# An attention and gated-convolution kernel on one core: loads as pieces of the written order, more buffers for them, and a new order for opening, period and end

## The chip, the cores and the metric

The kernel runs on one core of one Trainium2 chip. The metric is the device time of one execution in microseconds (us), lower is better.

## What is computed

```python
scores = q @ k^T / sqrt(64) + bias[head, distance]      # 8 sequences, 8 heads, 576 tokens, head size 64
scores = where(0 <= i - j < 128, scores, -1e9)          # window of 128 tokens back
attn   = exp(scores - max); attn /= sum(attn) + 1e-9
x      = (attn @ v), heads side by side                 # (8, 576, 512)
h      = relu(x @ w_in)                                 # w_in: 512 x 1024
c      = conv over tokens of h, 3 taps per column, zero at the ends of a sequence
out    = (h * sigmoid(c)) @ w_out                       # w_out: 1024 x 512
```

All inputs are float32. The 4608 tokens of the eight sequences are taken as one long row.

## The kernel before

**Units of work.** Tokens are cut into 36 tiles of 128 (index t). A tile's attention looks at the keys of the tile itself and of the one before it. Two tiles make a chunk of 256 tokens, of which there are 18; for each chunk the 1024 hidden columns are done in four steps of 256, so that there are 72 steps (index s). Both big products are made from three matmuls each, with every operand split in a high and a low part. The weights reach the kernel as words that must first be taken apart; there are 17 blocks of them (index b): 0 to 3 and 5 to 8 are the halves of `w_in`, 4 is the small convolution table, 9 to 16 are `w_out`.

**Pieces.** Nothing is left to a scheduler: the order of the instructions is written out as a string of pieces, and each engine runs its instructions in the order in which the pieces name them. A piece has a name, an index, and for some a half. The names, with the engine and the line of the work:

- weights, block b: F (load into a buffer `wst`, the sync engine SP, L152), CL (GpSimd, POOL, L159), RS (ScalarE, ACT, L164), V (VectorE, DVE, three instructions, L170 to L174), H (ACT, L182), P (TensorE, PE, L191 and L192), W (ACT, L196).
- attention, tile t: LD (loads of queries and keys into `rqk`, SP, L228), LV (load of values), Q (PE, transposes, L236), QO (ACT, copy, L240), S0 and S1 (PE, scores of four heads each, L262), MA (DVE, mask and bias, L278 and L291), RM (DVE, row extreme, L295), X (ACT, exponentials, L300), N (DVE, three instructions, L311 to L313), T (PE, transposes of the weights, L320), RL (ACT, L325), SEL (POOL, L331 and L334), AV (PE, L351), XH (ACT, L362), XL (DVE, L366), XF (DVE, the edge columns between chunks, L380 or L382).
- step s, with two halves of 128 columns: UH (PE, first product, 12 matmuls a half, L395), HH (ACT, relu, L403), Z (ACT, middle tap, L409), CV (DVE, the outer taps, L422), TH (ACT, tanh, L429), GT (DVE, gate, L433), GH (ACT, L440), GL (POOL, low part, L445), D (PE, second product, 12 matmuls, L459), OB (ACT copy, L469, and the store on SP, L471; only after the last step of a chunk).

A half is written after a point: N0.1 in the period below is the second half (heads 4 to 7) of the tile of that period. CV takes two instructions for a half, and four in the six chunks in which a sequence begins inside. The tiles in which a sequence begins or ends have one more mask instruction in each MA.

**Buffers.** `wst` has 3 buffers, `rqk` 2, the values 4. In PSUM five buffers (`pst`) are shared by Q, S, T, AV, P and UH; Z, CV and TH work on one buffer (`zp`), so that a step's Z waits for GT of the step before; D sums into two (`o`), which the next chunk can take only when OB has copied them. Z of a step's second half also waits for CV of its first, as both stand in the one buffer.

**Order.** `OPENING` carries tiles 0 to 5, all weights and steps 0 to 5. Then `PERIOD` is emitted once per tile for t = 6 to 39, with two steps each, and pieces whose tile or step does not exist are left out; so the last four rounds (t = 36 to 39) have only what is left: AV of tile 35 and the steps 66 to 71. Loads are not pieces. Eight are issued ahead of `OPENING`, and the others as part of a piece: V of block b issues F of block b + 3 (L177), Q of tile t issues LD of tile t + 2 (L479), AV of tile t issues LV of tile t + 3 (L488). They go into SP's one queue in that order, each waiting there until its buffer is free.

Of the kernel before, what the change touches and what calls it, by code (L numbers as in the profile page):

```python
# [21 lines left out]
def tile_alibi_window_attention_conv_glu(  # L22
# [144 lines left out]
    def w_bits(b):  # L167
        st, g = wst.pop(b), wgs[b]
        lo, hi = st[..., 0], st[..., 1]
        nc.vector.tensor_scalar(out=lo, in0=lo, scalar1=29, scalar2=None, op0=ALU.logical_shift_right)  # L170
        nc.vector.scalar_tensor_tensor(
            out=g, in0=g, scalar=3, in1=lo, op0=ALU.logical_shift_left, op1=ALU.bitwise_or
        )
# [346 lines left out]
    RM0.1 X0.0.0 RS2 H1 CL3 W0 P1 RS3 V2 X0.1.1 V3 S1.0 X0.0.1 X0.1.0 N0.0 MA1.0.0 H3 N0.1 MA1.0.1 T0.0  # L522
    CL4 S1.1 T0.1 RL0.0 RS4 P3 RM1.0 H2 P2 SEL0.0 MA1.1.0 RL0.1 CL6 SEL0.1 MA1.1.1 X1.0.0 X1.0.1 N1.0
    RM1.1 CL5 AV0 W2 T1.0 S2.0 V4 XH0 XL0 X1.1.0 X1.1.1 RL1.0 MA2.0.0 N1.1 RS5 H4 V5 SEL1.0 S2.1 P4 T1.1
    MA2.0.1 MA2.1.0 RM2.0 W3 MA2.1.1 H5 W1 RL1.1 CL7 XF0 SEL1.1 RS6 RS7 AV1 X2.0.0 V6 X2.0.1 W4 RM2.1 P5
    XH1 CL8 X2.1.1 V7 N2.0 Q4 RS8 X2.1.0 Q3 N2.1 V8 CL9 XL1 W5 QO4 XF1 H6 QO3 T2.1 H7 T2.0 P6 RL2.1
    RL2.0 RS9 CL10 S3.0 SEL2.0 SEL2.1 MA3.0.0 P7 S3.1 MA3.0.1 H8 AV2 MA3.1.0 P8 XH2 MA3.1.1 V9 W7 RM3.1
    CL11 XL2 RS10 RM3.0 XF2 UH0.0 RS11 V11 H9 UH1.0 X3.1.1 X3.0.0 V10 X3.1.0 H11 HH0.0 X3.0.1 HH1.0 N3.1
    UH0.1 S4.0 N3.0 MA4.0.0 CL12 Z0.0 T3.0 MA4.0.1 T3.1 HH0.1 CL14 Z0.1 RL3.0 P9 RL3.1 CV0.1 H10 RS12
    SEL3.0 W6 P10 RM4.0 SEL3.1 X4.0.1 AV3 W9 UH1.1 X4.0.0 CV0.0 CL13 P11 V12 N4.0 TH0 RS13 XH3 GT0 H12  # L530
    S4.1 XL3 W8 HH1.1 P12 Z1.0 MA4.1.0 XF3 GH0 Q5 Z1.1 MA4.1.1 UH2.0 CL15 GL0 CV1.1 W12 RM4.1 W10 QO5
    CV1.0 X4.1.0 X4.1.1 TH1 T4.0 V13 UH2.1 RS14 N4.1 HH2.0 H13 D0 GT1 V14 RL4.0 Z2.0 HH2.1 UH3.0 HH3.0
    CV2.0 T4.1 W11 Z2.1 CL16 GH1 CV2.1 RL4.1 P13 S5.0 MA5.0.0 UH3.1 GL1 TH2 GT2 S5.1 RS16 HH3.1 SEL4.1
    SEL4.0 GH2 MA5.1.0 RS15 Z3.0 D1 MA5.0.1 W13 V15 AV4 H14 XH4 Q6 RM5.0 H15 MA5.1.1 QO6 X5.0.0 Z3.1 XL4
    XF4 P15 P14 RM5.1 GL2 W14 X5.0.1 CV3.0 CV3.1 TH3 W15 V16 UH4.0 N5.0 D2 X5.1.1 H16 UH4.1 HH4.0 X5.1.0
# [53 lines left out]
```

## Time and profile before

| what | value |
|---|---|
| median of 3 runs | 698.07 us (697.06 to 699.02) |
| the profiled execution's own time | 697.87 us |
| its span in the trace | 696.1 us |
| TensorE (PE) busy | 654.1 us, 94% of the span |
| VectorE (DVE) busy | 521.1 us, 75% |
| ScalarE (ACT) busy | 444.1 us, 64% |
| GpSimd (POOL) busy | 191.5 us, 28% |
| TensorE clock, mean granted | 0.99 |

The profile is of one execution. A row of its timeline gives the start and the duration in us, the engine, the line, the operation and, in brackets, how long the engine stood idle before it and what ended that. Rows for the same line that follow one another are merged, with their count behind an x. A row of the chain of waits gives start, duration, engine and line of the work that ended last, followed back from the end. A row of the table by stretches gives for each engine the busy time and the instructions, then the granted TensorE clock as a share of full speed, and the DMA share. The profiled execution takes 1.8 us more than its span.

### The profile page before, as it was taken

To read this page: it belongs to the slowest core of one execution; us is meant where nothing else is said; L and a number is where in the kernel's file an instruction comes from. 1 tells how busy PE (TensorE), PEld (TensorE's weight loads), DVE (VectorE), ACT (ScalarE), POOL (GpSimd) and SP (SyncE) were. 2 spreads that over 40 slices of the span, in tenths; PEclk is the share of its full clock that TensorE was granted. 3 is DMA by queue.
4 is the path that set the end of the run, shared out by engine and by line. 5 is a ranking of instruction groups with operands and counts; after the bars stand their busy time and mean duration, and the time that the engine had idled before them with its cause. 6 is when DMAs were issued, how large, how long until landed. Compare 5 with 4: busy or idle time off the path is not lost.

```text
span 696.1 us, 13391 instructions
## 1 busy us (share of the span) xinstructions
PE 654.1 (94%) x4881; PEld 555.6 (80%) x4881; DVE 521.1 (75%) x1207; ACT 444.1 (64%) x1275; POOL 191.5 (28%) x234
## 2 busy tenths in 40 slices
...
GB/s 220 174 79 223 82 59 45 77 47 77 46 76 47 76 46 77 47 76 46 93 36 73 62 61 47 77 46 77 49 74 50 75 46 76 16 32 1 31 30 32
DMA packets 120101, 47.02 MB, mean 68 GB/s; under 512 B 113356, under 2 KB 113380, under 8 KB 120036
## 3 DMA queue, kind: packets, MB, share of 16 engines
...
## 4 chain that ended last, share of the span: by engine, by line
PE 52%; DVE 34%; ACT 8%; issue 3%; DMA 2%; SPq 1%; POOL 1%; ACTq 0%; DVEq 0%; POOLq 0%
PE o L459 18%; PE p L395 13%; DVE zp L422 10%; PE sc L262 7%; PE av L351 7%; DVE sc L278 5%; DVE st L295 4%; DVE e L313 4%; DVE e L291 4%; PE pa L320 3%; ACT zp L409 3%; PE pt L236 2%; DVE x L366 2%; DMA rqk<-in_k_dram 2%; PE pw L191 1%
## 5 line engine op out<-in xcount | busy, mean ns | idle before, releaser
L422 DVE SCALAR_TENSOR_TENSOR zp<-hh,cw,zp 128x256 f32<-128x256 f32 (+7 forms) x384 | 162.0, 422 | 89.8 <-ACT zp L409 81.3
L395 PE MATMUL p<-x,wi 128*128 128x258 f32 x1728 | 224.0, 286 | 2.8 <-DVE x L380 2.8
L395 PEld LDWEIGHTS p<-x,wi 128*128 128x128 f32 x1728 | 215.6, 191 | 8.8 <-issue 5.3
L459 PE MATMUL o<-wo,gh 128*128 128x512 f32 x576 | 188.2, 408 | 3.6 <-ACT ob L469 2.3
L300 ACT ACTIVATE e<-e,st 128x128 f32<-128x128 f32 x288 | 112.0, 391 | 33.7 <-DVE st L295 33.6
L459 PEld LDWEIGHTS o<-wo,gh 128*128 128x128 f32 x576 | 103.4, 189 | 30.5 <-issue 5.6
L445 POOL TENSOR_TENSOR gl<-z,gh 128x512 fp32r<-128x512 f32 x72 | 92.5, 1285 | 114.4 <-ACT gh L440 100.7
L331 POOL TENSOR_SCALAR_AFFINE_SELECT rl<-rl 128x512 f32<-128x512 f32 x64 | 40.6, 635 | 289.2 <-ACT rl L325 289.2
L459 PE MATMUL o<-wo,gl 128*128 128x512 f32 x288 | 114.8, 399 | 1.2 <-POOL gl L445 1.2
L409 ACT ACTIVATE zp<-hh,cw 128x256 f32<-128x256 f32 x144 | 69.1, 480 | 70.6 <-DVE zp L422 67.5
L403 ACT ACTIVATE hh<-p 128x258 f32<-128x258 f32 x144 | 54.7, 382 | 37.9 <-PE p L395 37.8
L433 DVE SCALAR_TENSOR_TENSOR z<-zp,hh 128x512 f32<-128x512 f32 x72 | 49.7, 690 | 34.1 <-ACT zp L429 34.1
L351 PEld LDWEIGHTS av<-rl,rv 128*64 128x64 f32 x1088 | 60.0, 139 | 12.9 <-POOL rl L334 9.2
L351 PE MATMUL av<-rl,rv 128*64 128x128 f32 x1088 | 69.3, 280 | 0.4 <-POOL rl L334 0.4
L262 PE MATMUL sc<-qkT_all 64*128 64x256 f32 x512 | 68.3, 395 | 0.5 <-DVE x L366 0.4
L459 PEld LDWEIGHTS o<-wo,gl 128*128 128x128 f32 x288 | 54.5, 189 | 15.3 <-POOL gl L445 2.1
L291 DVE SCALAR_TENSOR_TENSOR e<-sc,bias 128x256 f32<-128x256 f32 x144 | 61.2, 425 | 4.9
L262 PEld LDWEIGHTS sc<-qkT_all 64*128 64x128 f32 x512 | 48.3, 188 | 19.6 <-ACT zp L409 9.5
L320 PE MATMUL pa<-ident_r,e 128*128 128x128 f32 x288 | 42.5, 277 | 16.4 <-DVE e L313 12.1
L278 DVE COPY_PREDICATED sc<-m_prev,sc 128x256 f32<-128x256 uint8 x128 | 53.7, 420 | 5.2 <-PE sc L262 4.3
L362 ACT CAST x<-av 128x512 fp32r<-128x512 f32 x36 | 21.3, 591 | 56.5 <-PE av L351 56.5
L334 POOL TENSOR_SCALAR_AFFINE_SELECT rl<-rl 128x512 f32<-128x512 f32 x72 | 45.9, 638 | 39.7 <-ACT rl L325 28.8
...
## 6 DMA issues: line engine op xcount, KB each, us to landing
...
```

What stands on the lines that cost most here:

```text
L262: nc.tensor.matmul(pss[a][:, g], qt, qkT_all[rows, win, u, 1, g, :], start=True, stop=True)
L278: nc.vector.copy_predicated(out=s_cur, mask=mask.unsqueeze(1).to_broadcast(shp), data=data)
L291: nc.vector.scalar_tensor_tensor(out=heads, in0=s_cur, scalar=-0.125, in1=b, op0=ALU.mult, op1=ALU.add)
L300: nc.scalar.activation(out=e[:, j, :], in_=e[:, j, :], func=AF.Exp, bias=st[:, 0, j : j + 1], scale=-1.0, accum_out=st[:, 1, j : j + 1],)
L320: nc.tensor.transpose(ps[:, j, :], e[:, j, :], ident)
L351: nc.tensor.matmul(ps[a * D : (a + 1) * D, u * NG + g], vraw[tt][:, u * HU + j], rl[:, side, j], start=n == 0, stop=n == len(sides) - 1,)
L395: nc.tensor.matmul(ps[:, :XW], a[:, cc, f * P : (f + 1) * P], x[:, cc, :], start=n == 0, stop=n == last)
L403: nc.scalar.activation(out=hhs[s][:, ff, :], in_=pts.pop((s, ff, "up"))[:, :XW], func=AF.Relu, scale=0.5)
L409: nc.scalar.activation(out=zps[s][:, ff, :], in_=hhs[s][:, ff, 1 : 1 + CW], func=AF.Copy, scale=cw[:, 1, f : f + 1])
L422: nc.vector.scalar_tensor_tensor(out=z[:, ff, a:cut], in0=hh[:, ff, a + kk : cut + kk], scalar=cw[:, kk, f : f + 1], in1=z[:, ff, a:cut], ...
L445: nc.gpsimd.tensor_tensor(out=gl, in0=zgs.pop(s), in1=as32(gh), op=ALU.subtract)
L459: nc.tensor.matmul(oos[c][m], g[:, ff, ms], w[:, f, :], start=f == 0 and n == 0, stop=f == NFC - 1 and n == 2)
```

## The change

- `wst` gets 6 buffers instead of 3, `rqk` 3 instead of 2.
- F, LD and LV become pieces (`TILE` and `WEIGHT` name them), and V, Q and AV no longer issue any load.
- `OPENING` is another order of the same pieces, with the loads among them. `PERIOD` is another order, too.
- A third string, `TAIL`, is emitted once after the last period and takes the place of the four rounds with missing pieces.

```diff
     wpool = ctx.enter_context(tc.tile_pool(name="wpool", bufs=3))
+    NST = 6
...
-        st = wpool.tile([P, WB, 2], U32, name=f"wst{b}", tag="wst")
+        st = wpool.tile([P, WB, 2], U32, name=f"wst{b}", tag="wst", bufs=NST)
...
-        fetch_weight(b + 3)
...
-        rqk = apool.tile([P, 2, H, D], F32, name=f"rqk{t}", tag="rqk", bufs=2)
+        rqk = apool.tile([P, 2, H, D], F32, name=f"rqk{t}", tag="rqk", bufs=3)
...
-        if t + 2 < NT:
-            load(t + 2)
...
-    def attn_v(t):
-        av(t)
-        if t + 3 < NT:
-            loadv(t + 3)
...
+        "LD": load, "LV": loadv, "Q": qk, "QO": qk_out, "S": scores, "MA": merge, "RM": rowmax,
...
-    Q0 QO0 CL0 S0.0 Q1 MA0.0.0 RS0 MA0.0.1 V0 S0.1 MA0.1.0 RM0.0 MA0.1.1 QO1 CL1 Q2 H0 P0 CL2 QO2 RS1 V1
+    LD0 F0 LD1 LV0 F1 F2 F3 F4 LD2 LV1 F5 Q0 CL0 QO0 S0.0 S0.1 Q1 RS0 MA0.0.0 QO1 MA0.1.0 MA0.0.1
+    MA0.1.1 RM0.0 RM0.1 V0 F6 S1.0 X0.0.1 S1.1 X0.1.0 MA1.0.0 CL2 X0.1.1 N0.1 X0.0.0 T0.1 N0.0 MA1.0.1
...
     PERIOD = """
-    S0.0 S0.1 MA0.0.0 AV-1 MA0.0.1 D-2 OB-2 XH-1 XL-1 GH-1 RM0.0 X0.0.1 XF-1 MA0.1.0 UH0.0 MA0.1.1
-    X0.0.0 RM0.1 N0.0 UH0.1 GL-1 Q1 HH0.0 Z0.0 CV0.0 UH1.0 X0.1.0 HH0.1 Z0.1 X0.1.1 CV0.1 QO1 UH1.1 N0.1
-    T0.0 TH0 HH1.0 GT0 RL0.0 T0.1 HH1.1 SEL0.0 Z1.0 CV1.0 Z1.1 CV1.1 RL0.1 GH0 TH1 SEL0.1 D-1 OB-1 GT1
-    GL0
+    S0.0 S0.1 AV-1 LV2 MA0.0.0 XH-1 D-2 OB-2 MA0.0.1 XL-1 RM0.0 GH-1 X0.0.0 XF-1 UH0.0 X0.0.1 UH0.1
+    MA0.1.0 HH0.0 MA0.1.1 Z0.0 RM0.1 GL-1 UH1.0 CV0.0 HH0.1 X0.1.0 Z0.1 X0.1.1 N0.0 CV0.1 Q1 LD3 T0.0
+    UH1.1 N0.1 HH1.0 TH0 RL0.0 HH1.1 SEL0.0 GT0 Z1.0 T0.1 QO1 CV1.0 Z1.1 RL0.1 CV1.1 SEL0.1 GH0 TH1 GT1
+    GL0 D-1 OB-1
...
+    TAIL = """
+    AV-1 GH-1 XH-1 GL-1 XL-1 XF-1 D-2 OB-2 UH0.0 HH0.0 Z0.0 UH0.1 CV0.0 HH0.1 Z0.1 CV0.1 TH0 GT0 GH0 GL0
+    UH1.0 HH1.0 Z1.0 UH1.1 CV1.0 D-1 OB-1 HH1.1 Z1.1 CV1.1 TH1 GT1 GH1 GL1 UH2.0 HH2.0 Z2.0 UH2.1 CV2.0
...
+    CV5.0 D3 OB3 HH5.1 Z5.1 CV5.1 TH5 GT5 GH5 GL5 D4 OB4 D5 OB5
...
         emit(OPENING)
-        for t in range(FIRST, NT + 4):
+        for t in range(FIRST, NT):
             emit(PERIOD, t, 2 * (t - FIRST) + 6)
+        emit(TAIL, NT, 2 * (NT - FIRST) + 6)
```

Three places show what moves. Rows are instructions in the order of one engine: line, operation, what it writes and what it reads; the line numbers after the change are one or two lower.

The first is the order of VectorE early in the opening, from the second row extreme of tile 0 (`st_1`) on. Before:

```order
L295 TENSOR_REDUCE st_1_200<-e_1_199 128x4
L170 TENSOR_SCALAR wst_139<-wst_139 128x512
L171 SCALAR_TENSOR_TENSOR wg_241<-wg_241,wst_139 128x512
L174 SCALAR_TENSOR_TENSOR wg_241<-wst_139,wg_241 128x512
L170 TENSOR_SCALAR wst_191<-wst_191 128x512
L171 SCALAR_TENSOR_TENSOR wg_249<-wg_249,wst_191 128x512
L174 SCALAR_TENSOR_TENSOR wg_249<-wst_191,wg_249 128x512
L311 TENSOR_SCALAR st_0_181<-st_0_181 128x4
L312 RECIPROCAL st_0_181<-st_0_181 128x4
L313 TENSOR_TENSOR e_0_180<-e_0_180,st_0_181 128x512
L278 COPY_PREDICATED sc_0_0_263<-m_prev,sc_0_0_263 128x2x128
```

After:

```order
L293 TENSOR_REDUCE st_1_196<-e_1_195 128x4
L169 TENSOR_SCALAR wst_130<-wst_130 128x512
L170 SCALAR_TENSOR_TENSOR wg_187<-wg_187,wst_130 128x512
L173 SCALAR_TENSOR_TENSOR wg_187<-wst_130,wg_187 128x512
L276 COPY_PREDICATED sc_0_0_210<-m_prev,sc_0_0_210 128x2x128
L289 SCALAR_TENSOR_TENSOR e_0_226<-sc_0_0_210,bias 128x2x128
L309 TENSOR_SCALAR st_1_196<-st_1_196 128x4
L310 RECIPROCAL st_1_196<-st_1_196 128x4
L311 TENSOR_TENSOR e_1_195<-e_1_195,st_1_196 128x512
L309 TENSOR_SCALAR st_0_190<-st_0_190 128x4
L310 RECIPROCAL st_0_190<-st_0_190 128x4
L311 TENSOR_TENSOR e_0_189<-e_0_189,st_0_190 128x512
```

Before, four weight blocks (V0 to V3, the last two shown) stood ahead of N of tile 0 and MA of tile 1; now one does (V0, block `wst_130`), and MA and N of the two tiles come before V1.

The second is VectorE in one period, from the second row extreme on; `zp` is written by CV, `e` by N. Before:

```order
L295 TENSOR_REDUCE st_1_3646<-e_1_3645 128x4
L311 TENSOR_SCALAR st_0_3600<-st_0_3600 128x4
L312 RECIPROCAL st_0_3600<-st_0_3600 128x4
L313 TENSOR_TENSOR e_0_3599<-e_0_3599,st_0_3600 128x512
L422 SCALAR_TENSOR_TENSOR zp_3699<-hh_3697,cw,zp_3699 128x256 x4
L311 TENSOR_SCALAR st_1_3646<-st_1_3646 128x4
L312 RECIPROCAL st_1_3646<-st_1_3646 128x4
L313 TENSOR_TENSOR e_1_3645<-e_1_3645,st_1_3646 128x512
```

After:

```order
L293 TENSOR_REDUCE st_1_3674<-e_1_3673 128x4
L420 SCALAR_TENSOR_TENSOR zp_3681<-hh_3677,cw,zp_3681 128x256 x2
L309 TENSOR_SCALAR st_0_3619<-st_0_3619 128x4
L310 RECIPROCAL st_0_3619<-st_0_3619 128x4
L311 TENSOR_TENSOR e_0_3618<-e_0_3618,st_0_3619 128x512
L420 SCALAR_TENSOR_TENSOR zp_3681<-hh_3677,cw,zp_3681 128x256 x2
L309 TENSOR_SCALAR st_1_3674<-st_1_3674 128x4
L310 RECIPROCAL st_1_3674<-st_1_3674 128x4
```

N0.0 stood ahead of both halves of CV0; now it stands between them. On PE the period went UH0.0 UH0.1 Q1 UH1.0 UH1.1 T0.0 T0.1 and now goes UH0.0 UH0.1 UH1.0 Q1 T0.0 UH1.1 T0.1.

The third is the end of ScalarE's order, the last two steps (70 and 71). Before:

```order
L403 ACTIVATE hh_7923<-p_0_7892 128x258
L403 ACTIVATE hh_7923<-p_1_7909 128x258
L409 ACTIVATE zp_7928<-hh_7923,cw 128x256 x2
L440 CAST gh_7935<-z_7925 128x512
L429 ACTIVATE zp_7928<-zp_7928 128x512
L440 CAST gh_7966<-z_7951 128x512
L469 COPY ob_0_7982<-o_0_7842 128x512
L469 COPY ob_1_7985<-o_1_7843 128x512
```

After:

```order
L438 CAST gh_7899<-z_7897 128x512
L401 ACTIVATE hh_7916<-p_0_7903 128x258
L407 ACTIVATE zp_7918<-hh_7916,cw 128x256
L401 ACTIVATE hh_7916<-p_1_7920 128x258
L407 ACTIVATE zp_7918<-hh_7916,cw 128x256
L427 ACTIVATE zp_7918<-zp_7918 128x512
L438 CAST gh_7954<-z_7952 128x512
L467 COPY ob_0_7982<-o_0_7878 128x512
```

GH of step 70 (the first `gh` in each) stood behind the middle taps of step 71; now it stands ahead of all of step 71. On PE the end went UH68 UH69 D67 D68 UH70 UH71 D69 D70 D71, and now goes D66 UH69 D67 UH70 D68 UH71 D69 D70 D71.

More of the change, by code (lines that the diff above doesn't have):

```diff
@@ L483, in qk_out @@
             qkT_out(t, u)
-    def attn_v(t):
-        av(t)
-        if t + 3 < NT:
-            loadv(t + 3)
     TILE = {
-        "Q": qk, "QO": qk_out, "S": scores, "MA": merge, "RM": rowmax,
+        "LD": load, "LV": loadv, "Q": qk, "QO": qk_out, "S": scores, "MA": merge, "RM": rowmax,
         "X": lambda t, u, h: exps(t, u, range(2 * h, 2 * h + 2)),
-        "N": normal, "T": attnT, "RL": attn_out, "SEL": select, "AV": attn_v, "XH": x_hi, "XL": x_lo, "XF": xfin,
+        "N": normal, "T": attnT, "RL": attn_out, "SEL": select, "AV": av, "XH": x_hi, "XL": x_lo, "XF": xfin,
     }
@@ L502, in tile_alibi_window_attention_conv_glu @@
     }
-    WEIGHT = {"CL": w_clamp, "RS": w_rebias, "V": w_bits, "H": w_hi, "P": w_rest, "W": w_lo}
+    WEIGHT = {"F": fetch_weight, "CL": w_clamp, "RS": w_rebias, "V": w_bits, "H": w_hi, "P": w_rest, "W": w_lo}
     def emit(pieces, t=0, s=0):
@@ L520, in tile_alibi_window_attention_conv_glu @@
     OPENING = """
-    Q0 QO0 CL0 S0.0 Q1 MA0.0.0 RS0 MA0.0.1 V0 S0.1 MA0.1.0 RM0.0 MA0.1.1 QO1 CL1 Q2 H0 P0 CL2 QO2 RS1 V1
[L522 to L535, printed above, removed]
```

32 lines of the change are left out of this document (20 added, 12 removed).

## The prediction

> **What bounds the kernel now.** First the page, for the engine that is busy most; then the table by stretches, cut where the opening, the steady part and the end meet; then the waits of PE in each stretch.
>
> ```profile
> span 696.1 us, 13391 instructions
> PE 654.1 (94%) x4881; PEld 555.6 (80%) x4881; DVE 521.1 (75%) x1207; ACT 444.1 (64%) x1275; POOL 191.5 (28%) x234
> ```
>
> PE (TensorE) is busy for 94% of the span. The change takes no matmul away, so all that it can win lies in PE's other 42 us and in stretches at a lower clock. In the table the columns behind the stretch are its length and the busy time of PE, of its weight loads, DVE, ACT and POOL, then the granted clock, the DMA share and GB/s.
>
> ```profile
> 0.00:7.90 7.90, 3.36 (x16) 2.37 (x16) 3.17 (x20) 2.46 (x3) 1.60 (x10) 1.00 0.83 194
> 7.90:22.00 14.10, 6.99 (x27) 4.67 (x27) 6.30 (x14) 4.41 (x9) 1.92 (x3) 1.00 1.02 242
> 22.00:65.10 43.10, 32.66 (x192) 19.85 (x191) 37.85 (x82) 29.83 (x91) 12.75 (x19) 0.92 0.56 148
> 65.10:110.50 45.40, 44.32 (x294) 34.94 (x295) 39.56 (x85) 33.55 (x94) 12.69 (x16) 0.96 0.31 88
> 110.50:119.70 9.20, 9.20 (x62) 7.80 (x60) 6.05 (x13) 7.08 (x18) 2.92 (x4) 1.00 0.01 2
> 119.70:642.40 522.70, 512.60 (x4026) 448.22 (x4025) 410.54 (x964) 344.96 (x1019) 148.26 (x175) 1.00 0.24 58
> 642.40:696.10 53.70, 44.97 (x273) 37.72 (x272) 17.61 (x33) 21.79 (x46) 11.33 (x10) 0.97 0.08 30
> ```
>
> PE's idle time: 23.2 us in the opening (the first five rows: 119.7 less 96.5), 10.1 us in the 523 us of the steady part, 8.7 us in the end. DVE is the second engine in the opening: 37.85 of 43.1 us before the first step begins at 65.1. The waits of PE, in the steady part and from 630 us on (total, times, longest):
>
> ```profile
> PE pa L320 <- DVE e L313: 10.1, 19, 0.6
> ...
> PE o L459 <- ACT ob L469: 2.3, 1, 2.3
> PE o L459 <- ACT gh L440: 1.3, 2, 0.7
> PE o L459 <- POOL gl L445: 1.2, 2, 0.6
> ```
>
> The steady part has one kind of wait, T for N, in 19 tiles. So there are three separate sums.
>
> **The end (the tail order).** Here is what one wait costs, and how long a step takes from HH to the low part that D needs:
>
> ```profile
> 671.79 0.73 PE L459 MATMUL o<-wo,gh 128*128 128x512 f32 x2 [2.30 <-ACT ob L469]
> 673.66 1.06 PE L459 MATMUL o<-wo,gh 128*128 128x512 f32 x2
> 677.88 0.39 ACT L403 ACTIVATE hh<-p 128x258 f32<-128x258 f32 x1 [5.14 <-PE p L395]
> 679.93 0.48 ACT L409 ACTIVATE zp<-hh,cw 128x256 f32<-128x256 f32 x1 [0.22 <-DVE zp L422]
> 684.59 0.48 ACT L409 ACTIVATE zp<-hh,cw 128x256 f32<-128x256 f32 x1 [1.14 <-DVE zp L422]
> 687.56 0.62 ACT L440 CAST gh<-z 128x512 fp32r<-128x512 f32 x1 [0.83 <-DVE z L433]
> 688.26 1.30 POOL L445 TENSOR_TENSOR gl<-z,gh 128x512 fp32r<-128x512 f32 x1 [1.30 <-ACT gh L440]
> ```
>
> D68 starts a new chunk right behind D67 and waits 2.30 us for OB; then its pairs of matmuls take 1.06 us where they take 0.63 elsewhere, for nine more matmuls, some 1.8 us. Together with the other waits (1.3 + 1.2) and 0.15 us of refilling behind each of five, the end loses 2.3 + 1.8 + 2.5 + 0.7 = 7.3 us. In the new order a pair of UH stands between each two D up to D69, so OB of D67 is done under UH70, and the waits at D66, D68 and D70 go. What is late next: ACT, DVE and the one `zp` buffer. A step now runs alone, HH to GH. From HH of the first half to Z of the second is 679.93 − 677.88 = 2.05 us, from there to GH 687.56 − 684.59 = 2.97, GH itself 0.62: a step every 5.65 us. PE needs a UH pair and a D for each, 2.88 + 2.81 = 5.7 us (the chain's rows, below), so the two keep pace, but GH of a step stands ahead of HH of the next on ACT, and the chain begins late: UH67 follows UH66 at once. Counted on from there (end of UH66 = 0): GH66 ends at 4.3, HH67 starts then, HH71 at 4.3 + 4 × 5.65 = 26.9, its GH at 31.9, its low part is ready at 26.9 + 2.05 + 2.97 + 0.70 + 1.30 = 33.9. PE is through D70 at 31.3 (five more UH pairs, six D). So D71 waits 0.7 us for GH and about 1.4 more for GL: 2.1 us. The end gains 7.3 − 2.1 = **5.2 us** (7.3 if the chain is not late, 3.5 if it slips by half a microsecond more in each of the last steps).
>
> **The period.** One of the tiles whose CV takes four instructions, and, below the dots, one with the additional mask (its second RM, CV and T):
>
> ```profile
> 283.78 3.04 PE L395 MATMUL p<-x,wi 128*128 128x258 f32 x24
> 285.72 0.16 DVE L311 TENSOR_SCALAR st<-st 128x4 f32<-128x4 f32 x1
> 285.84 0.48 ACT L409 ACTIVATE zp<-hh,cw 128x256 f32<-128x256 f32 x1
> 286.13 0.69 DVE L313 TENSOR_TENSOR e<-e,st 128x512 f32<-128x512 f32 x1
> 286.66 1.03 PE L236 MATMUL pt<-ident_r,rqk 128*128 128x128 f32 x8
> 286.74 1.52 DVE L422 SCALAR_TENSOR_TENSOR zp<-hh,cw,zp 128x192 f32<-128x192 f32 x4
> 287.45 3.13 PE L395 MATMUL p<-x,wi 128*128 128x258 f32 x24
> 288.35 0.48 ACT L409 ACTIVATE zp<-hh,cw 128x256 f32<-128x256 f32 x1 [0.96 <-DVE zp L422]
> 288.86 1.53 DVE L422 SCALAR_TENSOR_TENSOR zp<-hh,cw,zp 128x192 f32<-128x192 f32 x4 [0.60 <-ACT zp L409]
> 291.55 0.63 PE L320 MATMUL pa<-ident_r,e 128*128 128x128 f32 x4 [0.53 <-DVE e L313]
> ...
> 250.38 0.69 DVE L295 TENSOR_REDUCE st<-e 128x4 f32<-128x512 f32 x1
> 253.61 1.01 DVE L422 SCALAR_TENSOR_TENSOR zp<-hh,cw,zp 128x256 f32<-128x256 f32 x2 [0.60 <-ACT zp L409]
> 255.78 0.63 PE L320 MATMUL pa<-ident_r,e 128*128 128x128 f32 x4 [0.56 <-DVE e L313]
> ```
>
> T0.1 waits for N0.1, and N0.1 comes behind CV0.0, Z0.1 and CV0.1. In the new order CV0.0 no longer waits for N0.0: it can start when Z0.0 is done (286.32 + 0.04) and ends at 287.9; N0.0 follows (from 285.72 to 286.82 before, some 1.05 us in a row) to 288.9, under which Z0.1 runs; CV0.1 starts at 288.9. Before, it started at 288.86. In these 12 tiles nothing changes: the 0.6 us in which DVE waited for Z are filled by N0.0, which has only been moved. T0.0 now stands before UH1.1 and is due at 283.78 + 2.88 (to 286.66, UH0) + 1.44 (half a UH more) + 0.8 (Q, 286.66 to 287.45) = 288.9, just as N0.0 ends; a short wait there costs nothing as long as T0.1 waits anyway.
>
> In the six tiles with the additional mask, RM0.1 ends only at 251.07, after Z0.0. Before: N0.0, CV0.0, then the 0.6 us wait for Z0.1, CV0.1 at 253.61. Now CV0.0 starts at 251.05 and N0.0 covers the wait: CV0.1 at 253.1, T0.1 at 255.25, when PE is due at 255.22. Six times 0.5 is 3.0 us. In the other eleven tiles, with CV of 1.0 us, the same steps from UH0.0 on give N0.1 ready at 7.0 us and PE due at 7.1: no wait, but a margin of 0.1 where there was 0.4. I charge 0.5 us for all of them together. ACT's copy of the next queries and keys (QO1, 1.04 us) now fills its gap between Z1.0 and Z1.1 and ends a microsecond before the next scores need it, so it costs nothing; were that margin gone, S0.0 would wait. Loads are issued earlier, and need 3 to 4 us of a period of 17. The period gains **2.5 us** (from 5 gained to 4 lost, if the eleven lose 0.3 each and the twelve 0.2).
>
> **The opening.** DVE's longest gap and the start of the first step, then the chain's rows for pieces of the later opening, and the first scores of tile 6:
>
> ```profile
> 21.82 0.69 DVE L171 SCALAR_TENSOR_TENSOR wg<-wg,wst 128x512 uint32<-128x512 uint32 x1 [6.86 <-ACT wg L164]
> 65.11 6.07 PE L395 MATMUL p<-x,wi 128*128 128x258 f32 x36 [2.81 <-DVE x L380]
> ...
> 104.19 0.86 PE pw L191 x2
> 105.28 0.86 PE pw L191 x2
> 110.61 2.88 PE p L395 x24
> 116.91 2.81 PE o L459 x12
> 119.72 1.93 PE sc L262 x16
> ```
>
> Before, ACT had Q2's copy ahead of RS1, and so DVE stood still for 6.86 us while tile 2's loads came in; the DMA is full then (share 1.02 from 7.9 to 22 us). In the new order LD2 has as many bytes ahead of it, so Q2 comes no earlier, but scores, masks, exponentials and N of tiles 0 and 1 stand ahead of it, and DVE works through. From 7.9 us to the UH of step 4 at 110.5 DVE was busy 6.30 + 37.85 + 39.56 = 83.7 of 102.6 us; 18.9 us were gaps. Step 4 needs XF4 (edge columns of chunk 1). CV3 (two times 1.01 us) now stands ahead of XF4, V15 and one RM (0.69) that stood ahead now stand behind it: some 83 us as before. Take 6.9 us from the gaps, and 1.6 for weight blocks that land earlier through six buffers, a choice: 10.4 us of gaps are left, and XF4 is done at 7.9 + 83 + 10.4 = 101.3 instead of 110.5.
>
> This gain is partly given back. PE now has more to do behind XF4: UH4 and UH5 (two pairs, 5.76), D2 and D3 (5.62), P15 and P16 (2 × 1.09) and T5 (two halves of 0.63 that overlap, 0.9), 14.4 us, where from UH4.0 to the scores of tile 6 it was 9.2. So S6.0 comes at 101.3 + 0.1 + 14.4 = 115.8 instead of 119.65, and DVE instead of PE is what PE waits for at UH4.0. The opening gains **3.8 us**: 8 if the gaps shrink to 6, a loss of 1.5 if only the 6.9 us gap goes and 3.5 us of new waits come (15.5 us of gaps, S6.0 at 121).
>
> For those new waits the row at 671.79 matters: a PE idle of 2.30 us is followed by matmuls at half speed, and the new opening leaves PE idle before 65 us as often as the old, so I left the half-speed stretches (clock 0.92 and 0.96 in the table) where they are. [...]
>
> **The sum.** 3.8 + 2.5 + 5.2 = 11.5 us off the profiled 697.87 (span 696.1 and 1.8 around it) is 686.4; the median of the runs is 0.2 higher, so **686.5 us**. Runs of this kernel can be told from no change at about 0.3%, 2.1 us.
>
> **The rivals.**
>
> - *The opening gives nothing* (0.22). SP takes the loads in the written order: LD4 stands behind F12, which waits until V6 has emptied its buffer, and Q4 stands ahead of UH0.0. If V6 comes at 47 us, LD4 lands at about 54, and UH0.0 wins little; and DVE paces steps 0 to 5 anyhow. For it: DVE is busy at 87% from 65 to 110 us. Against it: the gap of 6.86 us is filled for certain. Then 697.9 − 2.5 − 5.2 = 690.
> - *All of it works* (0.12). Opening 8, period 5, end 7: 678.
> - *The new period costs* (0.06). T0.0 is now due 2.2 us earlier against its UH0.0, and N0.0 comes behind CV0.0. If HH0.0, Z0.0 and CV0.0 take 0.7 us longer than the row at 286.74 lets me count, PE waits at T0.0 and then again at T0.1 in every one of 30 tiles. It decides from 0.45 us a tile on, which is what eats 9 us of the other two and 2.1 more. At 0.6 us a tile: 18 − 9 gives 707. Against it: Z0.0 ended 0.4 us before CV0.0 began, so the way is free.
> - *The change does nothing to the path* (0.04): loads were not what PE waited for, and both other strings lose in one place what they win in the other: 698.
>
> **The numbers.** The forecast has 0.56. Its own bounds reach from 681 to 692. With *the opening gives nothing* (690, and to 693 by the period's own bound) and most of *all of it works* inside, the range is 677 to 693; what it leaves out is the last two rivals and a little at the fast side. Faster by over 0.3%: 0.56 + 0.22 + 0.12 = 0.90; within 0.3%: 0.04; slower: 0.06.
>
> **What would show it.** In the changed profile: no wait of D for OB and none of D for GH but the last, of about 0.7, with 1.4 for GL; T waiting for N in 12 to 15 tiles, not in those with the additional mask; DVE without a gap of over 3 us between 8 and 22 us; UH0.0 before 60 us, a wait of PE for XF4 ahead of UH4.0, and S6.0 at 116. I am wrong if S6.0 comes later than 119.7, if T0.0 waits in most tiles, or if D70 still waits.

## The result, and the profile after

The changed kernel takes **679.29 us** (median of 3 runs, 678.99 to 680.48) where the kernel before takes 698.07: a ratio of 0.9736, with a 95% interval of 0.9707 to 0.9764, or 18.8 us less. Its profiled execution took 680.48 us with a span of 678.8 us, 17.3 us less than the span before. First the head of its page, then its table by stretches, cut as the table before (at UH0.0, UH4.0, the scores of tile 6 and the end of the last period).

```profile
span 678.8 us, 13359 instructions
PE 649.2 (96%) x4881; PEld 554.4 (82%) x4881; DVE 524.4 (77%) x1207; ACT 448.6 (66%) x1275; POOL 194.3 (29%) x234
```

```profile
0.00:7.90 7.90, 3.48 (x20) 2.78 (x22) 3.26 (x21) 2.69 (x4) 2.13 (x10) 1.00 0.83 200
7.90:22.00 14.10, 9.45 (x51) 6.93 (x48) 13.27 (x31) 9.05 (x32) 3.58 (x5) 0.78 0.93 262
22.00:54.80 32.80, 27.04 (x169) 16.62 (x167) 29.63 (x62) 23.12 (x65) 12.68 (x17) 0.89 0.63 173
54.80:96.90 42.10, 38.10 (x268) 29.83 (x269) 39.44 (x82) 31.41 (x80) 12.18 (x15) 1.00 0.49 104
96.90:111.30 14.40, 14.40 (x89) 11.93 (x87) 10.68 (x20) 10.97 (x34) 4.86 (x6) 1.00 0.01 2
111.30:628.70 517.40, 512.59 (x4025) 448.38 (x4024) 410.61 (x963) 349.49 (x1019) 147.47 (x174) 1.00 0.25 58
628.70:678.80 50.10, 44.15 (x273) 37.88 (x272) 17.56 (x33) 21.82 (x46) 11.37 (x10) 0.96 0.09 32
```

All three parts gain. The opening ends at 111.3 instead of 119.7 (−8.4), the steady part takes 517.4 instead of 522.7 (−5.3), the end 50.1 instead of 53.7 (−3.6): 17.3 together. PE's busy time in the steady part is the same to a hundredth (512.59 against 512.60), so what went there is idle time alone. In the second row DVE is now busy for 13.27 of 14.10 us, where it was 6.30.

**The opening.** The chain that ended last in the changed kernel, in its later opening (start, length, what): the first step's UH, the UH of step 4, and the scores of tile 6.

```profile
54.77 4.58 PE p L393 x36
...
93.94 2.99 PE o L457 x12
96.93 5.75 PE p L393 x48
102.69 2.81 PE o L457 x12
...
108.55 2.80 PE o L457 x12
111.34 0.84 PE sc L260 x5
```

UH0.0 starts at 54.77 instead of 65.11. UH4.0 (96.93) follows D1 at once: PE does not wait for the edge columns (XF4) in front of it. The waits of DVE from 7.9 us to UH4.0, in the kernel before and then in the changed one (total, times, longest):

```profile
DVE wg L171 <- ACT wg L164: 6.9, 1, 6.9
DVE sc L278 <- PE sc L262: 4.3, 5, 1.1
DVE sc L278 <- PE sc L260: 3.9, 2, 3.3
```

```profile
DVE sc L276 <- PE sc L258: 3.2, 1, 3.2
DVE sc L276 <- PE sc L260: 1.5, 2, 1.2
DVE x L364 <- ACT x L360: 0.4, 1, 0.4
```

Not only the gap of 6.9 us is gone. The masks' waits for scores (MA, the `sc` lines) were 8.2 us, 3.3 of them the wait for the very first scores; now that one is 3.2 (it ends at 7.81), and 1.5 instead of 4.9 us are left behind it.

**The period.** The waits of PE in the steady part, and one tile whose CV takes four instructions:

```profile
PE pa L318 <- DVE e L311: 4.8, 13, 0.4
```

```profile
291.31 4.48 PE L393 MATMUL p<-x,wi 128*128 128x258 f32 x36
...
293.37 0.48 ACT L407 ACTIVATE zp<-hh,cw 128x256 f32<-128x256 f32 x1
...
293.89 1.53 DVE L420 SCALAR_TENSOR_TENSOR zp<-hh,cw,zp 128x192 f32<-128x192 f32 x4 [0.53 <-ACT zp L407]
...
295.73 0.69 DVE L311 TENSOR_TENSOR e<-e,st 128x512 f32<-128x512 f32 x1
...
296.34 1.52 DVE L420 SCALAR_TENSOR_TENSOR zp<-hh,cw,zp 128x192 f32<-128x192 f32 x4
...
299.02 0.63 PE L318 MATMUL pa<-ident_r,e 128*128 128x128 f32 x4 [0.38 <-DVE e L311]
```

CV0.0 now waits 0.53 us for Z0.0, N0.0 fills the time of Z0.1, and CV0.1 (296.34) starts with no wait; T0.1 still waits, but 0.38 instead of 0.53. Thirteen waits are left of 19, the twelve of these tiles and one more. In the six tiles with the additional mask, T waits no more.

**The end.** PE at D71, then ACT and POOL on the last step:

```profile
669.57 0.74 PE L457 MATMUL o<-wo,gh 128*128 128x512 f32 x2 [1.50 <-ACT gh L438]
670.91 0.66 PE L457 MATMUL o<-wo,gl 128*128 128x512 f32 x1 [0.61 <-POOL gl L443]
671.37 1.05 PE L457 MATMUL o<-wo,gh 128*128 128x512 f32 x2
...
672.65 1.05 PE L457 MATMUL o<-wo,gh 128*128 128x512 f32 x2
...
674.66 0.39 PE L457 MATMUL o<-wo,gl 128*128 128x512 f32 x1
```

```profile
668.89 0.62 ACT L438 CAST gh<-z 128x512 fp32r<-128x512 f32 x1 [0.83 <-DVE z L431]
...
669.59 1.27 POOL L443 TENSOR_TENSOR gl<-z,gh 128x512 fp32r<-128x512 f32 x1 [4.24 <-ACT gh L438]
```

The only waits of PE behind the last UH are these two at D71, 2.11 us together. No D waits for OB any more. Behind the two waits the pairs of matmuls take 1.05 us instead of 0.63, as they did behind the 2.30 us wait of the kernel before.

### The profile page after: what moved, and what is told of

It reads as the page before. It is cut to its first block, busy times and chain, and to the rows that moved or that the text cites. A ratio compares the mean times of both kernels' runs of the same rounds, so it can differ in the third digit from the quotient of the medians.

```text
span 678.8 us, 13359 instructions
## 1 busy us (share of the span) xinstructions
PE 649.2 (96%) x4881; PEld 554.4 (82%) x4881; DVE 524.4 (77%) x1207; ACT 448.6 (66%) x1275; POOL 194.3 (29%) x234
## 4 chain that ended last, share of the span: by engine, by line
PE 71%; DVE 17%; issue 6%; ACT 3%; POOL 2%; DMA 1%; POOLq 0%; SPq 0%; DVEq 0%; ACTq 0%
PE o L457 27%; PE p L393 19%; PE av L349 9%; PE sc L260 8%; DVE zp L420 6%; PE pa L318 3%; DVE e L311 3%; PE pt L234 3%; DVE sc L276 1%; POOL gl L443 1%; DVE wg L170 1%; ACT zp L407 1%; PE pw L189 1%; DVE e L289 1%; DVE wg L173 1%
## 5 line engine op out<-in xcount | busy, mean ns | idle before, releaser
L457 PEld LDWEIGHTS o<-wo,gh 128*128 128x128 f32 x576 | 103.6, 189 | 27.4 <-issue 5.5
L329 POOL TENSOR_SCALAR_AFFINE_SELECT rl<-rl 128x512 f32<-128x512 f32 x64 | 41.5, 649 | 292.4 <-ACT rl L323 292.4
L260 PE MATMUL sc<-qkT_all 64*128 64x256 f32 x512 | 66.7, 391 | 2.9 <-ACT hh L401 1.5
L457 PEld LDWEIGHTS o<-wo,gl 128*128 128x128 f32 x288 | 54.4, 189 | 14.4 <-POOL gl L443 1.1
L427 ACT ACTIVATE zp<-zp 128x512 f32<-128x512 f32 x72 | 41.9, 582 | 31.5 <-DVE zp L420 19.5
L332 POOL TENSOR_SCALAR_AFFINE_SELECT rl<-rl 128x512 f32<-128x512 f32 x72 | 46.6, 647 | 38.4 <-ACT rl L323 23.4
L318 PE MATMUL pa<-ident_r,e 128*128 128x128 f32 x288 | 45.0, 280 | 10.3 <-DVE e L311 9.8
```

Source lines behind the costliest of these rows:

```text
L260: nc.tensor.matmul(pss[a][:, g], qt, qkT_all[rows, win, u, 1, g, :], start=True, stop=True)
L318: nc.tensor.transpose(ps[:, j, :], e[:, j, :], ident)
L457: nc.tensor.matmul(oos[c][m], g[:, ff, ms], w[:, f, :], start=f == 0 and n == 0, stop=f == NFC - 1 and n == 2)
```

## The experiments

The theory that was tested: the three parts act on three stretches and add up; the opening gains because DVE has work in its order that is ready while tile 2's loads come in, and because the weight loads run ahead; the period gains because N0.0 fills DVE's wait for Z0.1; the end gains because D no longer waits for OB. The main rival: the deeper buffers alone bring the loads forward, and the orders matter little. S6.0, the scores of tile 6, marks the end of the opening: 119.65 us before, 111.27 in the changed kernel (110.14 to 111.60 in the five profiled kernels that share its opening, itself among them). Ratios are against the kernel before, run on the same chip. Its medians in these comparisons are 697.14 to 698.07 us, so a difference from the 679.29 us of the changed kernel, taken apart from these runs, is good to about 1 us.

**1. The end alone.** The kernel before, with `TAIL` in place of its last four rounds.

```diff
-        for t in range(FIRST, NT + 4):
+        for t in range(FIRST, NT):
             emit(PERIOD, t, 2 * (t - FIRST) + 6)
+        emit(TAIL, NT, 2 * (NT - FIRST) + 6)
```

> The kernel before, with the new order for the end alone (its opening, period, buffers and loads are those of before). In the two traces the end, from AV of tile 35 on, went from 53.7 to 50.1 us. Theory: the end stands by itself, so 698.1 - 3.6 = 694.5, with a wait of D71 of about 2.1 us and matmuls at half speed behind it. Rival: the end gains only because the period ahead of it is another; then less than 1.5 us, 696.5 or more.

Measured: 692.83 us (692.11 to 693.96), ratio 0.993 [0.9909, 0.9952]; 4.7 us less than before on that chip (697.54), where 3.6 were expected. PE at its end:

```profile
682.73 0.74 PE L459 MATMUL o<-wo,gh 128*128 128x512 f32 x2 [1.50 <-ACT gh L440]
684.08 0.50 PE L459 MATMUL o<-wo,gl 128*128 128x512 f32 x1 [0.61 <-POOL gl L445]
684.41 0.63 PE L459 MATMUL o<-wo,gh 128*128 128x512 f32 x2
...
686.28 0.39 PE L459 MATMUL o<-wo,gl 128*128 128x512 f32 x1
```

The same waits, to a hundredth, but no half speed behind them: from the wait for GL to the end of the last matmul it is 2.6 us here (684.08 to 686.67) and 4.1 in the changed kernel (670.91 to 675.05). So the clock behind the wait costs 1.5 us in the profiled execution of the changed kernel, and nothing here, which makes up the larger gain. What decides between the two is not shown; the next section has what the traces say of it.

**2. The old opening.** The changed kernel with the opening, the buffers and the loads of before; its `PERIOD` (less LV2 and LD3, which the old Q and AV issue) and its `TAIL` stay.

```diff
-    NST = 6
...
-        st = wpool.tile([P, WB, 2], U32, name=f"wst{b}", tag="wst", bufs=NST)
+        st = wpool.tile([P, WB, 2], U32, name=f"wst{b}", tag="wst")
...
-        rqk = apool.tile([P, 2, H, D], F32, name=f"rqk{t}", tag="rqk", bufs=3)
+        rqk = apool.tile([P, 2, H, D], F32, name=f"rqk{t}", tag="rqk", bufs=2)
...
-        "LD": load, "LV": loadv, "Q": qk, "QO": qk_out, "S": scores, "MA": merge, "RM": rowmax,
+        "Q": qk, "QO": qk_out, "S": scores, "MA": merge, "RM": rowmax,
```

> The kernel before with the new period and the new end, but its own opening, three weight buffers, two for queries and keys, and loads issued as part of V, Q and AV. Theory: opening, period and end add up, so without the opening's 8.4 us the time is 698.1 - 5.3 - 3.6 = 689.2, and the first scores of tile 6 start at 119.7 us as before. Rival: the loads as pieces and the third buffer for queries and keys also help the steady part; then T or Q waits in the steady part and the time is over 691.

Measured: 688.42 us (688.13 to 688.85), ratio 0.9862 [0.9848, 0.9877], S6.0 at 119.08. The period and the end gain 9.1 us (697.54 − 688.42), and the opening the rest, 9.1 (688.42 − 679.29). The parts add up: the stretches of the profiles say 8.9 and 8.4.

**3. Three weight buffers.** The changed kernel with three buffers for weight words as before. The load F(b+3) stands behind V(b), where F(b+6) stood, F3 to F5 leave the top, and four clamps (CL4, 7, 8 and 15) that would now stand ahead of their load follow it at once.

```diff
-    NST = 6
+    NST = 3
...
-    LD0 F0 LD1 LV0 F1 F2 F3 F4 LD2 LV1 F5 Q0 CL0 QO0 S0.0 S0.1 Q1 RS0 MA0.0.0 QO1 MA0.1.0 MA0.0.1
+    LD0 F0 LD1 LV0 F1 F2 LD2 LV1 Q0 CL0 QO0 S0.0 S0.1 Q1 RS0 MA0.0.0 QO1 MA0.1.0 MA0.0.1 MA0.1.1 RM0.0
...
```

> The changed kernel with three weight buffers instead of six: F of block b + 3 stands behind V of block b (where F of b + 6 stood), F3 to F5 leave the top, and CL of blocks 4, 7, 8 and 15 move behind their loads; all else in the opening's order stays. Theory (the order won the opening): 0 to 2 us more, 679.3 to 681.5, since only blocks 7 and 8 would land later than VectorE wants them. Rival (the buffers won it): 4 us or more, 683 and up, with VectorE or POOL waiting for weight loads.

Measured: 693.61 us (692.93 to 695.02), ratio 0.9939 [0.9919, 0.9959], S6.0 at 123.50. That is 14.3 us slower than the changed kernel, so the expectation by the order alone fell. First ACT at RL0.0, the copy that SEL0.0 works on, then POOL at CL4 and SEL0.0 and at a later clamp, then PE at AV0:

```profile
21.39 0.56 ACT L323 COPY rl<-pa 128x512 f32<-128x512 f32 x1
```

```profile
24.78 0.58 POOL L158 TENSOR_SCALAR wst<-wst 24x128 f32<-24x128 f32 x1 [4.34 <-DMA wst<-in_moe_conv_w_dram]
25.31 0.62 POOL L332 TENSOR_SCALAR_AFFINE_SELECT rl<-rl 128x512 f32<-128x512 f32 x1
...
81.17 0.65 POOL L158 TENSOR_SCALAR wst<-wst 128x512 f32<-128x512 f32 x1 [10.25 <-DMA wst<-in_moe_w_out_dram]
```

```profile
25.99 1.97 PE L349 MATMUL av<-rl,rv 128*64 128x128 f32 x16 [3.97 <-POOL rl L332]
```

CL4 waits for the small block of convolution weights (its load now stands behind V1) and SEL0.0 stands behind it on POOL: 25.31 instead of 22.05, though RL0.0 is done at 21.95. AV0 on PE waits 3.97 us (0.39 in the changed kernel), some 3.4 of them (25.31 − 21.95) for the clamp. At 81.17 another clamp waits 10.25 us for its load. Two causes are mixed here, late weights and a clamp in the way, so the next two kernels part them.

**4. Three buffers, the clamps late.** As 3, but CL4, 7, 8 and 15 stand directly ahead of their RS, so that none of them holds up SEL.

```diff
-    V2 F8 LD3 LV2 AV0 X1.1.0 H1 T1.0 V3 F9 QO2 P1 RL1.0 S2.0 XH0 MA2.0.0 W0 XL0 CL6 H2
+    V2 F5 LD3 LV2 AV0 X1.1.0 H1 T1.0 V3 F6 QO2 P1 RL1.0 S2.0 XH0 MA2.0.0 W0 XL0 CL6 H2 X1.1.1 P2 W1 CL5
+    H3 CL4 RS4 SEL1.0 S2.1 MA2.0.1 RM2.0 RS5 N1.1 MA2.1.0 P3 X2.0.0 W2 RS6 W3 V4 F7 H4 V5 F8 P4 MA2.1.1
...
```

> The kernel with three weight buffers once more, but each CL that must follow a later load now stands as late as it can, directly ahead of its RS, so that on POOL no SEL of tiles 0 and 1 stands behind a CL that waits for a load. What it tells apart: if that queue on POOL cost the 14 us, most of it comes back, 683 or less. If the weights themselves come too late (F of b + 3 waits for V of b, a load and the two pieces between), VectorE or ScalarE still waits for them and the time is 688 to 694.

Measured: 688.73 us (687.74 to 689.51), ratio 0.9874 [0.9843, 0.9905], S6.0 at 121.47. Some 5 us (693.61 − 688.73) were the clamps' place; 9.4 (688.73 − 679.29) are left. ACT and PE wait for weights in a way that the changed kernel does not:

```profile
ACT wg L163 <- POOL wst L158: 19.1, 7, 8.4
```

```profile
PE pcw L186 <- DVE wg L173: 7.1, 1, 7.1
```

The first of these is 0.4 us in the changed kernel, the last 2.4. The clamps that ACT waits for wait themselves for their loads: 37.6 us on POOL between 7 and 112 us (27.4 and 10.2 for the two matrices), 12.5 in the changed kernel. With three buffers the new opening gains nothing over the old one (688.73 against 688.42; S6.0 is even 2.4 us later).

**5. Four weight buffers.** As the changed kernel, with F(b+4) behind V(b), and CL8 directly ahead of RS8.

```diff
-    NST = 6
+    NST = 4
...
-    LD0 F0 LD1 LV0 F1 F2 F3 F4 LD2 LV1 F5 Q0 CL0 QO0 S0.0 S0.1 Q1 RS0 MA0.0.0 QO1 MA0.1.0 MA0.0.1
+    LD0 F0 LD1 LV0 F1 F2 F3 LD2 LV1 Q0 CL0 QO0 S0.0 S0.1 Q1 RS0 MA0.0.0 QO1 MA0.1.0 MA0.0.1 MA0.1.1
...
```

> The changed kernel with four weight buffers: F of block b + 4 behind V of block b, and one CL (block 8) moved directly ahead of its RS. If the opening's order needs blocks early because several V stand close together, each buffer more takes off part of the loss: 681 to 687, between six buffers (679.3) and three. If only the loads behind the first three blocks matter (block 3 ahead of V0), four buffers are as good as six, 679 to 680.5.

Measured: 679.69 us (677.71 to 680.6), ratio 0.9744 [0.9715, 0.9772], S6.0 at 110.13. Four buffers are as good as six, so the price of too few is a step between three and four. The loads stand behind buffers in use all the same: on SP they wait for V for 28.6 us with six buffers and for 27.9 with four. What tells the depths apart is the wait of ACT's RS for the clamps: 0.4 us with six, 3.5 with four, 19.1 with three.

**6. Two buffers for queries and keys.**

```diff
-        rqk = apool.tile([P, 2, H, D], F32, name=f"rqk{t}", tag="rqk", bufs=3)
+        rqk = apool.tile([P, 2, H, D], F32, name=f"rqk{t}", tag="rqk", bufs=2)
```

> The changed kernel with two buffers for queries and keys instead of three; nothing else differs. In the opening of the changed kernel the loads LD2 and LD3 are issued at 9.2 and 27.1 us, when Q0 and Q1 have emptied their buffers anyway, so nothing there should wait; only LD7 would stand on SP until Q5 is done, with LV6 and LD8 behind it, which are needed much later. In the period the load of the tile three ahead stands directly behind the Q that empties its buffer. My theory (the third buffer is not what gains): 678.5 to 680.5, like the changed kernel. Rival (the third buffer lets the loads run ahead and carries part of the opening's 8 us): 682 or more, with a wait of T or S for queries or keys that is not there now.

Measured: 678.9 us (677.55 to 680.15), ratio 0.9745 [0.9712, 0.9777]. The third buffer for queries and keys gains nothing that can be measured.

**7. Q2 first.** In the changed opening, Q2 goes back ahead of S1.0 on PE, and its copies (QO2) ahead of the first exponentials on ACT, as in the order of before.

```diff
-    MA0.1.1 RM0.0 RM0.1 V0 F6 S1.0 X0.0.1 S1.1 X0.1.0 MA1.0.0 CL2 X0.1.1 N0.1 X0.0.0 T0.1 N0.0 MA1.0.1
-    CL1 T0.0 CL4 RS2 RL0.1 MA1.1.0 H0 RS1 RM1.0 Q2 MA1.1.1 SEL0.1 CL3 V1 F7 X1.0.0 X1.0.1 RM1.1 RL0.0 P0
+    MA0.1.1 RM0.0 RM0.1 V0 F6 Q2 S1.0 QO2 X0.0.1 S1.1 X0.1.0 MA1.0.0 CL2 X0.1.1 N0.1 X0.0.0 T0.1 N0.0
+    MA1.0.1 CL1 T0.0 CL4 RS2 RL0.1 MA1.1.0 H0 RS1 RM1.0 MA1.1.1 SEL0.1 CL3 V1 F7 X1.0.0 X1.0.1 RM1.1
```

> The changed kernel with one piece pair moved: Q2 stands ahead of the scores of tile 1 on TensorE, and QO2 ahead of the first exponentials on ScalarE, as in the kernel before. Theory (the gap of 6.9 us on VectorE was won by putting tiles 0 and 1 ahead of Q2): VectorE stands still again until tile 2's loads are in, 5 to 7 us, and the time is 684 to 686. Rival (VectorE's gap would have been made up later, as TensorE is the bound from the first step on): under 2 us more, 681 at most.

Measured: 685.46 us (684.04 to 688.41), ratio 0.9825 [0.9794, 0.9857], S6.0 at 116.38. PE stands at Q2, and DVE at the masks behind it:

```profile
16.87 0.66 PE L234 MATMUL pt<-ident_r,rqk 128*128 128x128 f32 x2 [6.35 <-DMA rqk<-in_q_dram]
```

```profile
21.55 0.43 DVE L276 COPY_PREDICATED sc<-m_prev,sc 128x256 f32<-128x256 uint8 x1 [6.57 <-PE sc L260]
```

Q2 and its copy in the wrong place bring a gap of 6.57 us back on DVE, and the opening ends 5.1 us later. So this opening needs both: the order that fills DVE while the loads come in, and at least four weight buffers. The order of before with more weight buffers was not run, so what the buffers give by themselves stays open.

**8. N0.0 first.** In the changed period, N0.0 goes back ahead of CV0.0 on DVE; PE's order stays.

```diff
-    MA0.1.0 HH0.0 MA0.1.1 Z0.0 RM0.1 GL-1 UH1.0 CV0.0 HH0.1 X0.1.0 Z0.1 X0.1.1 N0.0 CV0.1 Q1 LD3 T0.0
+    MA0.1.0 HH0.0 MA0.1.1 Z0.0 RM0.1 GL-1 UH1.0 N0.0 CV0.0 HH0.1 X0.1.0 Z0.1 X0.1.1 CV0.1 Q1 LD3 T0.0
```

> The changed kernel with N0.0 ahead of CV0.0 again on VectorE in the period, as before; TensorE's new order of the period stays. Theory (the wait of VectorE for Z0.1 is what N0.0 now covers in the six tiles with the additional mask): those six wait again, 0.7 us each with the refilling, and the other waits of T stay within 0.2 us, so 4 to 5 us more, 683 to 684.5. Rival (the gain of the period comes from T0.0 and UH1.1 on TensorE): under 1.5 us more.

Measured: 684.09 us (683.94 to 684.89), ratio 0.9809 [0.9787, 0.9831]. PE's waits in its steady part:

```profile
PE pa L318 <- DVE e L311: 6.5, 12, 0.6
PE pa L318 <- ACT rl L323: 3.8, 7, 0.6
```

All 19 waits are back, 10.3 us of them, and so are 4.8 us of time (684.09 − 679.29). In seven of them the profile names ACT as what came last. The swap of N0.0 and CV0.0 is what gains the period; with it undone, all else that is new in the period, the place of Q1 and UH1.1 on PE included, is worth 0.5 us (5.3 − 4.8), within the noise. The swap alone, in the period of before, was not run.

**9. The last wait of the period.** In the changed period D of the step before stands between T0.0 and T0.1 instead of behind T0.1: PE has 2.8 us of work that is ready while N0.1 ends.

```diff
-    UH1.1 N0.1 HH1.0 TH0 RL0.0 HH1.1 SEL0.0 GT0 Z1.0 T0.1 QO1 CV1.0 Z1.1 RL0.1 CV1.1 SEL0.1 GH0 TH1 GT1
-    GL0 D-1 OB-1
+    UH1.1 N0.1 HH1.0 TH0 RL0.0 HH1.1 SEL0.0 GT0 Z1.0 D-1 T0.1 QO1 CV1.0 Z1.1 RL0.1 CV1.1 SEL0.1 GH0 TH1
+    GT1 GL0 OB-1
```

> The changed kernel with one piece moved: in the period D of the step before stands ahead of T0.1 on TensorE instead of behind it. Theory (T0.1 waits only because N0.1 comes 0.4 us too late for it, and D has its operands long before): the 12 waits of 0.38 us and their refilling go, 4 to 6 us less, 673 to 675. Rival (what follows T0.1, the copy RL0.1 and the two selects on POOL, then comes late for AV of the next period): AV waits 0.3 us or more in most tiles and the time stays within 2 us or rises.

Measured: 676.14 us (674.82 to 676.55), ratio 0.969 [0.9667, 0.9712], 3.2 us less than the changed kernel. PE's waits in its steady part:

```profile
PE p L393 <- DVE x L378: 1.0, 2, 0.5
PE pa L318 <- DVE e L311: 0.3, 1, 0.3
```

Of the 4.8 us of waits 0.3 are left, and 1.0 is new, UH waiting for the edge columns (XF) where a chunk starts. The 12 waits were on the path, but the gain is a little less than their sum, and less than the 4 to 6 us that were expected.

**10. The last wait for GH.** In `TAIL`, HH and Z of a step's first half stand ahead of GH of the step before on ACT.

```diff
-    AV-1 GH-1 XH-1 GL-1 XL-1 XF-1 D-2 OB-2 UH0.0 HH0.0 Z0.0 UH0.1 CV0.0 HH0.1 Z0.1 CV0.1 TH0 GT0 GH0 GL0
-    UH1.0 HH1.0 Z1.0 UH1.1 CV1.0 D-1 OB-1 HH1.1 Z1.1 CV1.1 TH1 GT1 GH1 GL1 UH2.0 HH2.0 Z2.0 UH2.1 CV2.0
+    AV-1 GH-1 XH-1 GL-1 XL-1 XF-1 D-2 OB-2 UH0.0 HH0.0 Z0.0 UH0.1 CV0.0 HH0.1 Z0.1 CV0.1 TH0 GT0 UH1.0
+    HH1.0 Z1.0 GH0 GL0 UH1.1 CV1.0 D-1 OB-1 HH1.1 Z1.1 CV1.1 TH1 GT1 UH2.0 HH2.0 Z2.0 GH1 GL1 UH2.1
...
```

> The changed kernel, with HH and Z of a step's first half moved ahead of GH of the step before in the order for the end. Theory (the chain HH to GL is late because it starts one step behind, with GH ahead of the next HH): the chain catches up by step 69, D71 no longer waits (1.50 + 0.61 us), nor runs at half speed behind it; 2.1 to 3.5 us less, 675.8 to 677.2. Rival (the chain is bound by its own length, HH to GL 7.0 us against the 5.6 of D69 and D70): D71 still waits over 1 us and the gain is under 1 us.

Measured: 677.56 us (677.43 to 677.64), ratio 0.9713 [0.9692, 0.9734]. That is 1.7 us less than the changed kernel, where 2.1 to 3.5 were expected. D71 no longer waits for GH, but still for GL, and the pairs behind its one wait run at full speed:

```profile
669.56 0.50 PE L457 MATMUL o<-wo,gl 128*128 128x512 f32 x1 [0.62 <-POOL gl L443]
669.90 0.64 PE L457 MATMUL o<-wo,gh 128*128 128x512 f32 x2
```

**11. Both.** The edits of 9 and 10 together.

> The changed kernel with both edits, HH and Z first in the end and D ahead of T0.1 in the period. Theory: the two lie in different stretches and add up: 670 to 673. Rival: the period's edit gives nothing, and this is as fast as the end's edit alone, 676 to 677.

Measured: 673.40 us (671.58 to 673.87, 5 runs), ratio 0.9647 [0.9624, 0.967]. It is the fastest version, 5.9 us below the changed kernel; 9 and 10 alone gained 3.2 and 1.7. Their sum (4.9) is 1.0 less than 5.9, which is within what the time of the changed kernel, from another chip, may be off; so the two edits add up as far as can be told.

## Why the prediction was right, and where its sizes were off

The sign, the three separate sums and the mechanism of each held; the time came out 7.2 us below the forecast (679.3 against 686.5), inside the range but below the forecast's own bounds (681 to 692). The nearest of the recorded cases is the rival *all of it works* (678, chance 0.12): opening and period came out as it has them (8 and 5), the end did not (3.6, not 7). The terms miss by 4.6 and 2.8 us on one side and by 1.6 on the other, so part of the error cancelled. By terms, in the profiled executions (that of the changed kernel was 1.2 us slower than its median):

- **The opening: 3.8 forecast, 8.4 measured.** This is the term that was mis-sized, and within it the step "Take 6.9 us from the gaps, and 1.6 for weight blocks that land earlier": 10.4 us of gaps were to be left. DVE was busy for 82.3 us up to UH4.0 (13.27 + 29.63 + 39.44; forecast 83), but with gaps of 6.7 us. The long gap was not the only one that the new order fills; 3.4 us of the masks' waits for scores went with it, as the waits of DVE above show, and the rest in smaller pieces. That moves UH4.0 to 96.9, 4.4 us ahead of the forecast. Then PE took over where I had DVE as the last to arrive: PE came to UH4.0 straight from D1, with no wait for XF4. The other half of the step was right: from UH4.0 to S6.0 it took 14.4 us, as counted.
- **The rival *the opening gives nothing*** was wrong in the changed kernel, but it names what the opening hangs on: with three buffers (688.73) all of the gain is gone, with Q2 in its old place (685.46) most of it. My 1.6 us for the buffers was a choice that no row gave. Taken away from the finished order they cost 9.4; what they would give to the old order no run shows.
- **The period: 2.5 forecast, 5.3 measured.** The six tiles with the additional mask wait no more, as forecast, and their period fell by 0.73 us (17.90 to 17.17), not 0.5: 4.4 us. The wait itself was 0.56 us (the row at 255.78); the other 0.17 I put down to the refilling of PE behind it, an estimate. The 12 tiles with four CV instructions gained 0.08 each where I had nothing, about 1 us. The 0.5 us that I charged to the other eleven was not paid. T0.0 waits in no tile, so the rival *the new period costs* has nothing behind it. Two of its numbers were wrong as well: T0.0 comes 1.4 us earlier against its UH0.0, not 2.2 (290.42 − 283.78 before, 296.57 − 291.31 now), and 9 us and 2.1 more in 30 tiles are 0.37 us a tile, not 0.45.
- **The end: 5.2 forecast, 3.6 measured.** D66 to D70 wait for nothing, and D71 waits 2.11 us where 2.1 was forecast. The split was off (1.50 for GH and 0.61 for GL, not 0.7 and 1.4), because D's first pair reads all of GH: PE waits for its end (668.89 + 0.62 = 669.51), and I had put its start there. What I left out is the half speed behind the wait. I had counted it for the kernel before (1.8 us behind 2.30) and not for my own new wait: 1.5 us, and 5.2 − 1.5 is 3.7. Experiment 1 has the same order of the end and the same waits without the half speed, so these two alone do not bring the loss (below). No run shows the 0.15 us of refilling that my 7.3 us count behind each wait; in experiment 1 the first pair behind the wait for GH took 0.74 us and the later ones 0.63, a difference of 0.11.
- **The clock in the opening.** I left the half-speed stretches (clock 0.50) where they were. In the changed kernel there are two of 6.8 us, from 15.74 to 22.57 and from 36.22 to 43.05, 13.7 us together, where before it was 10.2. This is not shown to come from the new order: the kernel of experiment 11 has the same opening, with a mean clock of 0.95 in its first 110.8 us where the changed kernel has 0.94. Nor did the lower clock make the opening longer (S6.0 at 111.27 in the changed kernel, at 111.59 in that of experiment 11); DVE, busy for 13.27 of 14.10 and 29.63 of 32.80 us, sets the pace there. Near the starts of the two stretches PE has these waits, of 4.16 and 2.35 us; that they bring the half speed is not shown:

```profile
16.66 2.21 PE L318 MATMUL pa<-ident_r,e 128*128 128x128 f32 x8 [4.16 <-DVE e L311]
...
35.21 0.21 PE L186 MATMUL pcw<-ident_r,wg 24*128 24x24 f32 x1 [2.35 <-DVE wg L173]
```

**The clock at the end.** Ten kernels of this record have the same two waits at D71, 1.5 and 0.6 us, and what follows them is not the same. In the changed kernel the table by stretches has a clock of 0.54 there (the third number from the end), and the pairs take 1.05 us:

```profile
671.30:674.80 3.50, 3.50 (x10) 2.58 (x8) 0.00 (x0) 0.58 (x1) 0.00 (x0) 0.54 0.14 53
```

So do the pairs of D71 in the kernel of experiment 2, where in that of experiment 1 they take 0.63 (the rows from 684.41 on), and the clock stays at 1.00 up to 684.80:

```profile
678.72 0.57 PE L459 MATMUL o<-wo,gl 128*128 128x512 f32 x1 [0.63 <-POOL gl L445]
679.09 1.05 PE L459 MATMUL o<-wo,gh 128*128 128x512 f32 x2
...
680.37 1.05 PE L459 MATMUL o<-wo,gh 128*128 128x512 f32 x2
```

So the waits and the order of the end, the same in these three, do not decide it, and what does is not shown. The order for the end is worth 3.6 us with the half speed, as profiled, and by my estimate some 5.1 us (3.6 + 1.5) without.
